# Where the products of the 64-key remainders with v stand in an attention and feed-forward kernel, and where their weights are kept

## The chip, the cores and the metric

The kernel runs on one core of a Trainium2 chip. A core has a matrix engine (PE, with weight loads PEld beside its matmuls), a vector engine (DVE), a scalar engine (ACT), a third elementwise engine (POOL) and queues that issue transfers (here SP's). Each engine works through a list of its own in order; engines wait for one another by semaphores. The metric is the device time of one execution, in microseconds (us).

## The reference

Eight batches of twelve heads, 448 tokens, head width 64. Attention uses a sigmoid in place of a softmax; the heads side by side are the 768 columns of x, which goes through two matrix products with g = h - tanh(h) between them.

```python
def _attn_ref(q, k, v):
    scale = 1.0 / np.sqrt(q.shape[-1])
    scores = scale * np.matmul(q, k.transpose(0, 1, 3, 2)) - np.log(S)
    attn = 1.0 / (1.0 + np.exp(-scores))
    return np.matmul(attn, v).astype(np.float32)

def _moe_ref(x, w_in, w_out):      # (3584, 768) x (768, 2048) x (2048, 768)
    h = x @ w_in
    g = h - np.tanh(h)
    return (g @ w_out).astype(np.float32)
```

A sigmoid needs no sum over the keys, so the products of weights and v can be added up in any order, key block by key block.

## The kernel before

**Numbers.** Most products are made of two f16 halves of each f32 operand: high by high, low by high, high by low, three matmuls for one. The halves of the attention weights ("ahl") are made by `split_a`: the high one on ACT (L411), the low one on DVE (L412). From batch 2 on (`AV32 = 2`) the attention runs this way; batches 0 and 1 take v and the weights in f32.

**Pairs and key blocks.** Heads are taken two by two: pair j (0 to 5) of a batch fills 128 of x's columns, one head in each half. The 448 keys are three blocks of 128 (c = 0, 1, 2) and a remainder of 64 (c = QT = 3). The remainders of an even pair g and the odd pair h = g + 1 are computed together, so that the array is used as four parts of 64x64: `scores` with two pairs and `av` with two accumulators. The other scores use two parts of 64 rows by 128 columns, the other products with v two parts of 128 rows by 64 columns, and the matmuls of the feed-forward part the whole array.

**The attention as a stream.** `stream` is a generator that lays out the attention of batches 1 to 7. One turn of its loop handles two pairs g and h, in four steps between which it yields:

- step 1: scores of (g, 0) and (g, 1) and their sigmoids on ACT (`units`, `weigh`, L405); then `do_av`, the products with v that are in the list `todo`: (h, 0..2) of the turn before, after which that h is closed; then `keep` splits the two new blocks of weights; loads and the squares of v (`norm_v`, L335)
- step 2: scores of (g, 2) and of the remainder (g, QT), sigmoids, norms of k and q, splits
- step 3, behind a short piece with the scales of the next two pairs (`pbn`, L344): scores of (h, 0), (h, 1); `do_av` for (g, 0..2) and the remainder, which opens h's accumulator; g is closed; the halves of the next v's and k's; splits
- step 4: scores of (h, 2), sigmoid, split

Closing a pair (`close_acc`, `evac_x`) copies its accumulator to x on ACT (L439) and takes squares (`add_squares`): for j = 0 and 5 on ACT (L454), for the others a product on POOL (L456), and for j = 1 to 4 the running sum on POOL too (L465), the last of which is `x2b`. There are two accumulators in PSUM, one under the tag "av" for even pairs, which also holds `pbn`, and one under "tr" for odd pairs.

**The order around it.** `second(b)` runs the second feed-forward product of batch b (`moe2`, L857) unit by unit: a unit is six matmuls, sixteen units make one tile of 128 tokens, and 48 units the batch's three tiles; the remainder of 64 tokens (`por`, L905, two parts of 128x64) follows. A tile has two accumulators `po`, for the two halves of the columns, and there are two such buffers in all, so that the next tile begins when ACT (L890) and DVE (L894) have copied the last one out; in batch 1's first tile ACT makes both copies (L890, L892). `BLOCKS` says behind which unit the next step of the stream is laid out:

```python
BLOCKS = (8, 11, 16, 20, 20, 20, 27, 32, 36, 36, 36, 43, 48, 52, 52)
```

These are step 4 (8), 1 (11), 2 (16), the scales, 3 and 4 (20, 20, 20), 1 (27), 2 (32), scales, 3 and 4 (36), 1 (43), 2 (48), scales and 3 (52). Steps 2 thus stand where a token tile ends. The step behind unit 43 is the first of the next batch's attention, and it closes the last pair of the present one; three units later the sums over x's squares (`token_norms`, `nm`, L690) are laid out, and then x's halves (L723, L724). Batch 1 has a list with three more steps (4, 7, 8, 11, 13, 16, ...), in which step 1 comes at unit 13. The first feed-forward product (`moe1`, L773) has no attention beside it. The engines' lists are in this order, which is written out by hand.

**Room.** The tile `wo` holds w_out's halves, 32 slots of 768 f16 columns, and three slots more, through which the f32 numbers were moved while they were split; `scratch` gives parts of it by offset. Splits of weights otherwise take buffers of the common pool "t" (eight).

Of the kernel before, what the change touches and what calls it, by code (L numbers as in the profile page):

```python
# [8 lines left out]
F16 = mybir.dt.float16  # L9
# [10 lines left out]
P = 128  # L20
D = 64
QT = 3
# [11 lines left out]
class Builder:  # L34
# [286 lines left out]
    def load_v(self, b, j, pool, tag, bufs):  # L321


        at = 0 if j % 2 == 0 else 2 * QT + 2
        n = 2 * QT + (0 if j % 2 else 2)
        t = pool.tile([P, n, D], F32, name="vn", tag=tag, bufs=bufs)
        self.nc.sync.dma_start(t, self.v[b, j // 2, :, at : at + n])
        return t
# [76 lines left out]
        self.nc.scalar.activation(a[:, 0], ps[:, :, : self.S], AF.Sigmoid, bias=self.nls, scale=scale)  # L405
        return a

    def split_a(self, a):
        nc = self.nc
        A = self.tp.tile([P, 2, 2, self.S], F16, name="ahl", tag="t")  # L410
        nc.scalar.activation(A[:, 0], a[:, 0], AF.Copy, scale=A_SCALE)  # L411
        nc.vector.scalar_tensor_tensor(A[:, 1], a[:, 0], A_SCALE, A[:, 0], op0=ALU.mult, op1=ALU.subtract)  # L412
        return A

    def av(self, acc, v, A, c, odd):


        half = c == QT
        m = P // len(acc)
        prods = ((0, 0), (1, 0), (0, 1)) if A.dtype == F16 else ((0, 0),)  # L420
        for n, (w, x) in enumerate(prods):
            for i in range(len(acc)):
                for h in range(2):
                    k = slice(i * m, (i + 1) * m)
                    self.nc.tensor.matmul(  # L425
                        acc[i][h * D : (h + 1) * D, : self.S],
                        v[k, w, 2 * QT + h if half else h * QT + c],
                        A[k, x, h],
                        start=(n == 0 and (i == 1 if half else c == 0 and not odd)),
                        stop=(n == len(prods) - 1 and (i == 0 if half else c == QT - 1 and bool(odd))),  # L430
                    )

    def evac_x(self, j, acc, iv):
# [34 lines left out]
    def stream(self):  # L468

        NP = self.NP
        G = (self.B - 1) * NP
        at = lambda g: (1 + g // NP, g % NP)
        splits = lambda g: at(g)[0] >= self.AV32
        qk, vn, sc, K, Q, vv, accs = {}, {}, {}, {}, {}, {}, {}

        def load(g):
            if g < G and g not in qk:  # L480
                qk[g] = self.load_qk(*at(g))

        def load_v(g):
            if g < G and splits(g):
                vn[g] = self.load_v(*at(g), self.nat, "vn", 2)

        def sums(g):
            ss = self.sums[g // 2 % 2]
            return ss if splits(g) else ss[:, :4]

        def norms(g):
            if g < G:
                for n, t in enumerate(qk[g]):
                    self.norm(t, sums(g)[:, 2 * n + g % 2 : 2 * n + g % 2 + 1])

        def norm_v(g):
            if g in vn:
                self.norm(vn[g], sums(g)[:, 4 + g % 2 : 5 + g % 2])

        def scales(g, where):  # L500
            if g < G:
                sc[g] = sc[g + 1] = self.scales(sums(g), where)

        def parts_k(g):
            if g < G:
                K[g] = self.parts(qk[g][0], sc[g][0][:, 0:1], "K", not splits(g) and g not in (2, 3))

        def parts_q(g):
            if g < G:
                Q[g] = self.parts(qk[g][1], sc[g][0][:, 1:2], "Q", True)  # L510
                qk.pop(g)

        def prep_v(g):
            if g >= G:
                return
            if splits(g):
                vv[g] = self.prep_v(vn.pop(g), sc[g][0])
            else:
                vv[g] = self.load_v(*at(g), self.att, "vhl", 3)[:, None]

        load(0)
        load(1)
        yield 0, False
        norms(0)
        norms(1)
        yield 0, False
        scales(0, "tr")
        yield 0, False
        parts_k(0)
        yield 450, False  # L530
        parts_q(0)
        load(2)
        yield 450, False
        parts_k(1)
        yield 450, False
        parts_q(1)
        load(3)
        yield 450, False
        norms(2)
        yield 0, False  # L540
        todo = []

        def open_acc(g):
            tag = "tr" if g % 2 else "av"
            accs[g] = self.ps.tile([P, 512], F32, name="acc", tag=tag, bufs=1)
            if g % NP == 0:
                self.xs = []

        def close_acc(g):
            iv = sc[g][1][:, 1:2] if splits(g) else None  # L550
            self.xs.append(self.evac_x(g % NP, accs.pop(g), iv))
            if g % 2:
                vv.pop(g - 1)
                vv.pop(g)
            for d in (sc, K, Q):
                d.pop(g)

        def do_av():
            for g, c, A in todo:
                odd = g % 2  # L560
                if c == QT:
                    open_acc(g + 1)
                    self.av([accs[g], accs[g + 1]], vv[g], A, c, odd)
                    close_acc(g)
                    continue
                if c == 0 and not odd:
                    open_acc(g)
                self.av([accs[g]], vv[g], A, c, odd)
                if c == QT - 1 and odd:
                    close_acc(g)  # L570
            todo.clear()

        def units(g, cs, between=lambda: None):

            pss = []
            for c in cs:
                n = 2 if c == QT else 1
                pss.append(self.scores([K[g + i] for i in range(n)], [Q[g + i] for i in range(n)], c))
            aa = [self.weigh(pss[0], sc[g][1][:, 0:1])]
            between()  # L580
            aa += [self.weigh(ps, sc[g][1][:, 0:1]) for ps in pss[1:]]
            return aa

        def keep(g, cs, aa):
            if splits(g):
                aa = [self.split_a(a) for a in aa]
            todo.extend((g, c, a) for c, a in zip(cs, aa))

        for g in range(0, G, 2):
            h = g + 1  # L590
            early = g == 0

            aa = units(g, (0, 1))
            do_av()
            if early:
                prep_v(0)
                prep_v(1)
            keep(g, (0, 1), aa)
            load(g + 3)
            norm_v(g + 2)  # L600
            norm_v(g + 3)
            yield 2750, True

            aa = units(g, (2, QT))
            if early:
                do_av()
            norms(g + 3)
            keep(g, (2, QT), aa)
            yield 2750, True

            if not early:
                scales(g + 2, "av")
                parts_k(g + 2)
                yield 0, False

            aa = units(h, (0, 1), (lambda: None) if early else lambda: parts_q(g + 2))
            do_av()
            if early:
                yield 2750, True
                scales(g + 2, "mm")  # L620
                parts_k(g + 2)
                parts_q(g + 2)
            prep_v(g + 2)
            keep(h, (0, 1), aa)
            prep_v(g + 3)
            load(g + 4)
            load_v(g + 4)
            load_v(g + 5)
            yield 2750, True

            aa = units(h, (2,), lambda: parts_k(g + 3))
            if early:
                do_av()
            keep(h, (2,), aa)
            parts_q(g + 3)
            norms(g + 4)
            yield 2750, True
        do_av()
        yield 1150, True

    def attention32(self):
# [497 lines left out]
```

## Time and profile before

| | us |
|---|---|
| median of the runs | 1165.48 |
| lowest run | 1165.2 |
| the profiled execution | 1166.29 |
| its span, from the first to the last instruction | 1164.5 |
| mean granted TensorE clock | 0.999 |
| one turn of the attention loop, from step 1 to step 1 (574.29 to 599.07) | 24.8 |

The time line of an engine merges neighbouring instructions of one line. Its columns are the start, how long the group took, the engine, the line of the kernel, the operation, the tile written and the tiles read, the shape (for matmuls first the part of the array: rows by columns), and their count; in brackets stands the idle time ahead of the group and what ended it. Matmuls overlap, so a group's length is a little more than the distance to the next group's start.

### The profile page before, as it was taken

Reading aid. Unit: us, or ns where it says so; the run is one execution under the profiler, and the core shown is the slowest. Engines: PE = TensorE matmul, PEld = TensorE weight load, DVE = VectorE, ACT = ScalarE, POOL = GpSimd, SP = SyncE. Lnnn points to the kernel's source line nnn. Section 1 sums busy time; section 2 is a strip of 40 time slices with the busy share of each in tenths; the row PEclk is TensorE's granted clock in tenths of the full one; section 3 lists DMA queues with packets and bytes.
Section 4 is the critical chain, followed back from the end, with each engine's and each line's share of the span. In section 5 each row is a group of like instructions: output and inputs, shape, how many; then the busy total and the mean of one; then the engine's idle time right before and its main releaser. Section 6 shows DMA issues by size and latency. Waiting matters only on the chain.

```text
span 1164.5 us, 18896 instructions
## 1 busy us (share of the span) xinstructions
PE 1153.1 (99%) x7563; PEld 597.4 (51%) x7564; DVE 907.7 (78%) x1308; ACT 865.5 (74%) x1195; POOL 79.1 (7%) x58
## 2 busy tenths in 40 slices
PE   9999999999999999999999999999999999999998
PEld 3345444555555555555555555555555555555565
DVE  6999999789777996679867897778976798646930
ACT  7988996588976888768887688867887688745820
POOL 0000000000120002200021000200022000300000
PEclk9999999999999999999999999999999999999999
DMA  9942171000222002210022101210012100000000
GB/s 358 357 163 64 42 224 53 29 7 1 80 75 64 7 1 78 62 53 1 17 76 62 40 1 31 82 58 24 1 55 84 53 1 9 23 28 7 1 14 35
DMA packets 34056, 70.43 MB, mean 60 GB/s; under 512 B 3888, under 2 KB 21040, under 8 KB 33968
## 3 DMA queue, kind: packets, MB, share of 16 engines
q1 hardware_dynamic: 33744, 68.89, 18.1%
q8 instruction: 59, 0.97, 0.4%
q10 hardware_dynamic: 224, 0.33, 0.1%
q14 instruction: 29, 0.24, 0.1%
HBM read 58.20 MB, written 11.01 MB: 59 GB/s over the span
## 4 chain that ended last, share of the span: by engine, by line
PE 73%; ACT 1%; issue 0%; DVE 0%; ACTq 0%
PE ph L773 28%; PE po L857 27%; PE sc L394 6%; PE acc L425 6%; PE por L905 5%; ACT a L405 0%; ACT ahl L411 0%; PE nm L690 0%; ACT sqn L335 0%; ACT x L439 0%; ACT Q L369 0%; DVE orem L914 0%; PE pbn L344 0%; ACT x L454 0%; ACT o L892 0%
## 5 line engine op out<-in xcount | busy, mean ns | idle before, releaser
L857 PE MATMUL po<-wo,g 128*128 128x384 f16 x2304 | 389.1, 326 | 3.1 <-DVE wo L240 1.6
L773 PE MATMUL ph<-xhl,wi 128*128 128x448 f16 x2016 | 382.6, 352 | 0.0
L857 PEld LDWEIGHTS <-g 128*128 128x128 f16 x2304 | 220.3, 98 | 170.1 <-issue 26.4
L773 PEld LDWEIGHTS <-wi 128*128 128x128 f16 x2016 | 196.7, 98 | 185.0 <-issue 2.1
L412 DVE SCALAR_TENSOR_TENSOR ahl<-a,ahl 128x896 f16<-128x896 f32 x126 | 162.7, 1326 | 125.6 <-ACT ahl L411 125.0
L405 ACT ACTIVATE a<-sc,nls,rn 128x896 f32<-128x896 f32 x147 | 155.8, 1090 | 37.4 <-PE sc L394 37.2
L811 ACT ACTIVATE u<-ph,ih 128x896 f32<-128x896 f32 x64 | 64.4, 1006 | 75.8 <-PE ph L773 74.0
L411 ACT ACTIVATE ahl<-a 128x896 f16<-128x896 f32 x126 | 113.2, 941 | 0.6
L394 PE MATMUL sc<-Q,K 64*128 64x448 f16 x1008 | 100.8, 353 | 0.9 <-DVE th L816 0.7
L815 DVE SCALAR_TENSOR_TENSOR m<-ph,ihk,u 128x896 f32<-128x896 f32 x64 | 73.5, 1149 | 25.6 <-ACT th L813 25.2
L766 ACT ACTIVATE g<-m,Sg 128x896 f16<-128x896 f32 x64 | 66.7, 1041 | 35.5 <-DVE m L829 28.5
L829 DVE COPY_PREDICATED m<-u,th 128x896 f32<-128x896 uint32 x64 | 77.2, 1206 | 6.8 <-ACT u L828 0.8
L425 PE MATMUL acc<-ahl,vhl 128*64 128x448 f16 (+1 forms) x864 | 80.6, 356 | 0.4 <-ACT tn L346 0.4
L456 POOL TENSOR_TENSOR x<-x 128x448 f32<-128x448 f32 x24 | 28.3, 1178 | 762.1 <-ACT x L439 762.1
L767 DVE SCALAR_TENSOR_TENSOR g<-m,Sg,g 128x896 f16<-128x896 f32 x64 | 73.4, 1147 | 6.8 <-ACT g L766 6.7
L826 DVE SCALAR_TENSOR_TENSOR m<-q,m 128x896 f32<-128x896 f32 x64 | 69.9, 1092 | 6.7 <-DVE m L822 0.5
L983 PE MATMUL ph<-x,wi 128*128 128x448 f32 x192 | 73.8, 540 | 0.0
L816 DVE SCALAR_TENSOR_TENSOR th<-ph,ih,th 128x896 f32<-128x896 f32 x64 | 73.3, 1145 | 0.0
L822 DVE SCALAR_TENSOR_TENSOR m<-q,m 128x896 f32<-128x896 f32 x64 | 69.6, 1087 | 0.0
L828 ACT ACTIVATE u<-u,b 128x896 f32<-128x896 f32 x64 | 66.7, 1042 | 1.9
L821 ACT ACTIVATE q<-u,b 128x896 f32<-128x896 f32 x64 | 65.8, 1028 | 0.0
L825 ACT ACTIVATE q<-u,b 128x896 f32<-128x896 f32 x64 | 65.8, 1028 | 0.0
(141 smaller groups left out, 1087.7 us busy)
## 6 DMA issues: line engine op xcount, KB each, us to landing
knn<-k SPq DMA_DIRECT2D x45, 224.0 KB, 2.6
qnn<-q SPq DMA_DIRECT2D x44, 224.0 KB, 2.6
rawo<-moe_w_out SPq DMA_DIRECT2D x22, 384.0 KB, 5.2
out<-o SPq DMA_DIRECT2D x21, 384.0 KB, 2.3
raw<-moe_w_in SPq DMA_DIRECT2D x13, 512.0 KB, 8.2
vn<-v SPq DMA_DIRECT2D x24, 256.0 KB, 2.8
wo<-moe_w_in SPq DMA_DIRECT2D x11, 512.0 KB, 8.3
vn<-v SPq DMA_DIRECT2D x24, 192.0 KB, 2.4
```

Of the source, the lines that this page charges most:

```text
L394: self.nc.tensor.matmul(ps[i * m : (i + 1) * m, h, : self.S], K[i][r, w, c * P : c * P + m], Q[i][r, x, :], start=(n == 0), stop=(n == len ...
L405: self.nc.scalar.activation(a[:, 0], ps[:, :, : self.S], AF.Sigmoid, bias=self.nls, scale=scale)
L411: nc.scalar.activation(A[:, 0], a[:, 0], AF.Copy, scale=A_SCALE)
L412: nc.vector.scalar_tensor_tensor(A[:, 1], a[:, 0], A_SCALE, A[:, 0], op0=ALU.mult, op1=ALU.subtract)
L425: self.nc.tensor.matmul(acc[i][h * D : (h + 1) * D, : self.S], v[k, w, 2 * QT + h if half else h * QT + c], A[k, x, h], start=(n == 0 and ...
L767: nc.vector.scalar_tensor_tensor(g[:, 1], m, Sg, g[:, 0], op0=ALU.mult, op1=ALU.subtract)
L773: self.nc.tensor.matmul(ph, self.wi[:, self.slot(c, k), part, e * P : (e + 1) * P], xhl[c][:, x, :], start=(i == 0), stop=(i == len(prods) ...
L815: V.scalar_tensor_tensor(m, ps, ihk, u, op0=ALU.mult, op1=ALU.mult)
L816: V.scalar_tensor_tensor(th, ps, ih, th, op0=ALU.mult, op1=ALU.subtract)
L829: V.copy_predicated(m, u.bitcast(U32), th)
L857: nc.tensor.matmul(po[i][:, :H], gs[f // 2][:, x, f % 2, tk * P : (tk + 1) * P], self.wo[:, i * self.NF + 2 * ks[f // 2] + f % 2, w], star ...
L983: nc.tensor.matmul(ph[:, e, :S], self.fp32(self.wi, self.slot(c, k))[:, 0, e * P : (e + 1) * P], xs[c], start=(c == 0), stop=(c == self.NC ...
```

## The change

From batch 2 on, the scores of the remainder (g, QT) move from step 2 to step 1, and the products of that remainder with v move from step 3 of the same turn to step 1 of the next turn, directly behind the remainder scores of the next two pairs, which use the array in the same four parts. Step 1 now has scores (g, 0); the products (h, 0..2) of the turn before; scores (g, QT); the remainder products of the turn before (`do_rest`), which close both of its pairs. Step 2 has scores (g, 1) and (g, 2). The weights of a remainder are used a turn after they are made; their halves lie in the three last slots of `wo`, in one place for all turns. The 64 remainder rows of v now lie with the odd pair's blocks (first six and then eight columns of 64, in place of eight and six), and the accumulation of a pair starts with block c = 0 and stops with the remainder.

```diff
     def load_v(self, b, j, pool, tag, bufs):
-        at = 0 if j % 2 == 0 else 2 * QT + 2
-        n = 2 * QT + (0 if j % 2 else 2)
+        first = 2 * QT + (2 if b < self.AV32 else 0)
+        at = j % 2 * first
+        n = 4 * QT + 2 - first if j % 2 else first
@@
-    def split_a(self, a):
-        nc = self.nc
-        A = self.tp.tile([P, 2, 2, self.S], F16, name="ahl", tag="t")
+    def split_a(self, a, kept):
+        nc = self.nc
+        if kept:
+            A = self.scratch((self.NF - self.SHIFT_O) * 2 * self.HALF, 4 * self.S).rearrange("p (x h n) -> p x h n", x=2, h=2)
+        else:
+            A = self.tp.tile([P, 2, 2, self.S], F16, name="ahl", tag="t")
@@
-    def av(self, acc, v, A, c, odd):
+    def av(self, acc, v, A, c, odd, late=False):
         half = c == QT
+        if late:
+            begin, end = (not half and c == 0,) * 2, (half,) * 2
+        else:
+            begin = (False, True) if half else (c == 0 and not odd,)
+            end = (True, False) if half else (c == QT - 1 and bool(odd),)
@@
-                        start=(n == 0 and (i == 1 if half else c == 0 and not odd)),
-                        stop=(n == len(prods) - 1 and (i == 0 if half else c == QT - 1 and bool(odd))),
+                        start=(n == 0 and begin[i]),
+                        stop=(n == len(prods) - 1 and end[i]),
@@
+        def do_rest():
+            while kept:
+                g, A = kept.pop()
+                self.av([accs[g], accs[g + 1]], vv[g + 1], A, QT, 0, True)
+                close_acc(g)
+                close_acc(g + 1)
+
         def do_av():
             for g, c, A in todo:
                 odd = g % 2
+                if splits(g):
+                    if c == 0:
+                        open_acc(g)
+                    self.av([accs[g]], vv[g], A, c, odd, True)
+                    continue
@@
         def keep(g, cs, aa):
             if splits(g):
-                aa = [self.split_a(a) for a in aa]
-            todo.extend((g, c, a) for c, a in zip(cs, aa))
+                aa = [self.split_a(a, c == QT) for c, a in zip(cs, aa)]
+            for c, a in zip(cs, aa):
+                if splits(g) and c == QT:
+                    kept.append((g, a))
+                else:
+                    todo.append((g, c, a))
@@
-            aa = units(g, (0, 1))
-            do_av()
+            first, second = ((0, QT), (1, 2)) if splits(g) else ((0, 1), (2, QT))
+            if splits(g):
+                aa = units(g, (0,))
+                do_av()
+                aa += units(g, (QT,))
+                do_rest()
+            else:
+                aa = units(g, first)
+                do_av()
@@
-            keep(g, (0, 1), aa)
+            keep(g, first, aa)
@@
-            aa = units(g, (2, QT))
+            aa = units(g, second)
@@
-            keep(g, (2, QT), aa)
+            keep(g, second, aa)
@@
         do_av()
+        do_rest()
```

Outside the chip the array v is laid out in the matching order before it is passed in.

More of the change, by code (lines that the diff above doesn't have):

```diff
@@ L540, in stream @@
         yield 0, False
-        todo = []
+        todo, kept = [], []
         def open_acc(g):
@@ L1122 @@
     rest = v[:, :, QT * P :].reshape(B, H // 4, 2, 2, D, D).transpose(0, 1, 2, 4, 3, 5).reshape(B, H // 4, P, 2, D)
+    n = Builder.AV32
+    v_first = np.concatenate([heads[:n, :, :, 0], rest[:n], heads[:n, :, :, 1]], axis=3)
+    v_later = np.concatenate([heads[n:, :, :, 0], heads[n:, :, :, 1], rest[n:]], axis=3)
     arrays = {
@@ L1125 @@
         "k": pairs(k),
-        "v": np.ascontiguousarray(np.concatenate([heads[:, :, :, 0], rest, heads[:, :, :, 1]], axis=3)),
+        "v": np.concatenate([v_first, v_later]),
         "moe_w_in": np.ascontiguousarray(moe_w_in).view(np.uint64),
```

## The prediction

> **What bounds the kernel now.** I read the page's busy times first, then the table of windows, then the waits, and last each engine's time line around one turn of the attention loop.
>
> ```profile
> PE 1153.1 (99%) x7563; PEld 597.4 (51%) x7564; DVE 907.7 (78%) x1308; ACT 865.5 (74%) x1195; POOL 79.1 (7%) x58
> 500.00:600.00 100.00, 100.00 (x660) 52.68 (x656) 85.71 (x114) 76.44 (x97) 6.12 (x4) 1.00 0.10 30
> ```
>
> In the window row the columns behind the length are PE, PEld, DVE, ACT, POOL, clock, DMA share and GB/s: PE is at work for all of these 100 us, at the full clock. So the change can act in two ways only: PE's own work gets shorter or longer, or PE is made to wait where it waits for nothing today. Moving work between the other engines costs nothing until one of them is late for PE.
>
> **The change part by part.** *The shapes on PE.* The number of matmuls stays. What changes is how often PE goes from one array shape to another: full (w_out's products), 64 rows (scores, "S"), 64 columns (products with v, "A"), 64x64 (both remainders, "R").
>
> ```profile
> 574.29 1.31 PE L394 MATMUL sc<-Q,K 64*128 64x448 f16 x12
> ...
> 582.33 1.43 PE L394 MATMUL sc<-Q,K 64*128 64x448 f16 x18
> ...
> 588.95 2.58 PE L425 MATMUL acc<-ahl,vhl 128*64 128x448 f16 x30
> 591.47 0.74 PE L394 MATMUL sc<-Q,K 64*128 64x448 f16 x6
> 592.14 7.00 PE L857 MATMUL po<-wo,g 128*128 128x384 f16 x42
> 599.07 1.31 PE L394 MATMUL sc<-Q,K 64*128 64x448 f16 x12
> 600.31 1.89 PE L425 MATMUL acc<-ahl,vhl 128*64 128x448 f16 x18
> 602.13 5.05 PE L857 MATMUL po<-wo,g 128*128 128x384 f16 x30
> 607.12 1.43 PE L394 MATMUL sc<-Q,K 64*128 64x448 f16 x18
> 608.48 4.08 PE L857 MATMUL po<-wo,g 128*128 128x384 f16 x24
> ```
>
> From start to start, 12 S take 1.24 us (599.07 to 600.31) and 6 S take 0.67 (591.47 to 592.14), so six more cost 0.57 and a stretch of its own 0.10. 18 A take 1.82, which is 3 x 0.57 + 0.11. The 30 of 588.95 are 18 A and 12 R, 2.52: the R cost 0.70, that is 0.57 + 0.13; the 18 of 607.12 are 6 S and 12 R, 1.36, and give 0.69. One change of shape costs 0.10 to 0.13; I take 0.12. The new order has one meeting without a row, A followed by S (steps 3 and 4); it is bounded by these ends.
>
> Changes of shape in a turn: before, step 1 has 3 (S A full), step 2 has 3 (S R full), steps 3 and 4 have 5 (S A R S full); after, 4 (S A R full), 2 and 4. One fewer. Where a batch's remainder tokens (L905, the shape of A) surround steps 2 and 3, which is so in the first turn of batches 3 to 7, it is two fewer. The last remainder of all needs one more. 18 turns: 12 x 1 + 1 (batch 2's first) + 5 x 2 - 1 = 22, times 0.12 = 2.6 us saved. Within a turn step 1 grows by 0.70 (12 R for 6 S, and 12 more R), step 2 shrinks by 0.13, steps 3 and 4 by 0.69.
>
> *What else moves to step 1.* Both pairs of the turn before are now closed there: two copies of x on ACT (L439) and up to four POOL instructions (L456, L465) come together, where before the even pair's stood in step 3. The second sigmoid now waits on ACT for R scores which stand behind A, and the copies and both splits (L411) are queued behind it. The split's other half on DVE (L412) collides with POOL, and behind it on DVE stands the copy of w_out's result (L894), for which PE's next token tile waits: `po` has two buffers, and both are in use. That is the chain to work out.
>
> ```profile
> 576.54 2.07 ACT L405 ACTIVATE a<-sc,nls,rn 128x896 f32<-128x896 f32 x2
> 578.50 0.62 ACT L439 ACTIVATE x<-acc,rn 128x448 f32<-128x448 f32 x1
> ...
> 599.85 2.09 ACT L405 ACTIVATE a<-sc,nls,rn 128x896 f32<-128x896 f32 x2 [2.32 <-PE sc L394]
> 602.24 0.64 ACT L439 ACTIVATE x<-acc,rn 128x448 f32<-128x448 f32 x1 [0.30 <-PE acc L425]
> 602.78 1.78 ACT L411 ACTIVATE ahl<-a 128x896 f16<-128x896 f32 x2
> ...
> 627.03 0.63 ACT L439 ACTIVATE x<-acc,rn 128x448 f32<-128x448 f32 x1 [0.30 <-PE acc L425]
> 627.75 0.58 ACT L454 ACTIVATE x<-x 128x448 bf16<-128x448 f32 x1
> ```
> ```profile
> 166.71 1.14 POOL L465 TENSOR_TENSOR x<-x,x 128x448 f32<-128x448 f32 x1 [9.15 <-ACT x L454]
> ...
> 579.27 0.94 POOL L456 TENSOR_TENSOR x<-x 128x448 f32<-128x448 f32 x1 [96.08 <-ACT x L439]
> 580.28 1.86 POOL L465 TENSOR_TENSOR x<-x,x 128x448 f32<-128x448 f32 x1
> ```
> ```profile
> 574.09 0.45 DVE L371 TENSOR_SCALAR K<-knn,sn 128x448 f16<-128x448 f32 x1
> ...
> 576.17 0.68 DVE L372 SCALAR_TENSOR_TENSOR Q<-qnn,sn,Q 128x448 f16<-128x448 f32 x1
> 580.00 3.09 DVE L412 SCALAR_TENSOR_TENSOR ahl<-a,ahl 128x896 f16<-128x896 f32 x2 [3.14 <-ACT ahl L411]
> 583.01 0.60 DVE L894 TENSOR_SCALAR o<-po,iK 128x384 f32<-128x384 f32 x1
> 587.19 2.09 DVE L412 SCALAR_TENSOR_TENSOR ahl<-a,ahl 128x896 f16<-128x896 f32 x2 [3.57 <-ACT ahl L411]
> ```
>
> Two splits on DVE take 2.09 us alone and 3.09 beside POOL, and POOL's sum takes 1.86 beside DVE and 1.14 where it went first: they take turns, and a split that waited ends 0.95 after POOL's instruction (580.28 + 1.86 = 582.14, and 580.00 + 3.09 = 583.09). ACT's next begins 1.0 after a sigmoid, 0.53 after an x, 0.85 after a split; POOL begins 0.14 after x ends.
>
> *Turn at 599.07 (step 1 behind unit 27).* A sigmoid starts 0.78 after its scores (599.85). R scores start at 599.07 + 0.67 + 1.82 = 601.56, their sigmoid at 602.37, the x copies at 603.37 and 603.90, the splits at 604.43 and 605.28, ending 605.38 and 606.23. POOL: product 604.14, sum 605.15 to 606.29. The first DVE split, ready at 605.4, ends at 607.2, POOL's next product at 608.0, the second split at 609.0, the copy L894 at 609.5. PE: step 2 starts at 607.12 + 0.70 = 607.82, the next tile at 609.06, its second product at 609.22. A wait of 0.3 us; six times, 1.9.
>
> *Turn at 574.29 (behind unit 11).* ACT is later from the start (576.54). R sigmoid 577.58, first x 578.58, its square on ACT (j = 0; 0.09 behind x, 0.58), second x 579.8 to 580.4, splits to 581.25 and 582.1. POOL's product runs 580.54 to 581.48, the split ends 582.4, POOL's sum 583.4, the second split 584.4, L894 584.9; PE wants it at 582.33 + 0.70 + 1.24 + 0.16 = 584.43. A wait of 0.5; five times, 2.5. Q's low half for the R scores (L372, to 576.85) is just in time for their second product (574.29 + 2.49 + 0.21 = 576.99): nothing, at most 0.1 a turn if late.
>
> ```profile
> 623.85 1.31 PE L394 MATMUL sc<-Q,K 64*128 64x448 f16 x12
> ...
> 629.85 0.35 PE L690 MATMUL nm<-x2b,onesb 128*128 128x448 bf16 x1
> ```
>
> *Turn at 623.85 (behind unit 43).* The sums nm of line 690 need POOL's last sum, which today follows step 3 and is long done. After: R sigmoid 623.85 + 2.49 + 0.81 = 627.15, x 628.15 to 628.78, product 628.92, sum 629.94 to 631.08 (DVE has nothing ready to collide). PE is there at 629.85 + 0.70 = 630.55: a wait of 0.6, five times, 3.0; the last batch has no sigmoid in front, 0.15.
>
> ```profile
> 301.07 1.31 PE L394 MATMUL sc<-Q,K 64*128 64x448 f16 x12
> ```
> ```profile
> 302.79 2.07 ACT L405 ACTIVATE a<-sc,nls,rn 128x896 f32<-128x896 f32 x2
> ...
> 308.07 0.57 ACT L890 ACTIVATE o<-po,iK 128x384 f32<-128x384 f32 x1
> 308.54 0.58 ACT L892 ACTIVATE o<-po,iK 128x384 f32<-128x384 f32 x1
> ```
>
> *Batch 1's first tile.* Step 1 comes at unit 13, three units before the tile ends, and both copies of the result are on ACT. The R sigmoid starts at about 301.07 + 2.49 + 0.81 = 304.4 at the earliest, where today's second starts at 303.8, and an x and a square (0.53 + 0.6) come in between: 1.7 us later, while PE is 0.6 later. Net 1.1 to 1.7 with late Q halves; I take 1.5.
>
> *At no cost:* the loads of v (same bytes, swapped between the pairs, a turn ahead); the kept halves in w_out's room, written in step 1 and read by PE a turn (24.8 us) later, their reader of the turn before being through before the R sigmoid ends; one buffer of the common pool fewer in use.
>
> *Sum:* -2.6 + 1.9 + 2.5 + 3.15 + 1.5 = +6.5 us. The profiled execution took 1166.29 (span 1164.5), which becomes 1172.8; on the median 1165.48, 0.8 below it, 1172.0. The waits have ends: 0.2 to 0.8 behind unit 11, 0 to 0.6 behind 27, 0.4 to 0.8 at nm, 0.6 to 2 in batch 1, so 3.7 to 13.6 together, and +1 to +11 net.
>
> *A rule weighed.* L894 reads PSUM and never lies beside POOL here. Its 0.60 for 384 elements is slower than L371's 0.45 for 448 from SBUF, which speaks for another way of reading; behind unit 27 POOL's last sum is waiting just then, and if L894 had to take its turn it would end 0.95 later. I take none of it. The Trainium skill, SBUF — State Buffer, section "Who interferes with whom", says that a DVE instruction with at most one SBUF input outside the two-port modes does not contend with GpSimd; by it the sum is my +6.5, without it +12.2; no run here shows it yet.
>
> **The rivals.** (1) *The waits don't arise, only the saved changes count:* 1165.5 - 2.6 = 1162.9. For it: the waits are 0.3 to 0.6, small beside the 3 to 5 us chains they are worked out from. Against it: at nm PE needs a chain of sigmoid, x and two POOL instructions that ends 0.6 late without any collision. (2) *L894 takes turns with POOL:* six times 0.95 more, 1177.7. (3) *PE waits for the kept halves although it doesn't read them*, because they are written into the tile wo which every product of w_out reads: then the first product behind step 1 waits for the second split, 609.0 - 602.83 = 6.2 us in the turn at 599.07, 18 times, less 2.6: 1274, slower. It decides from 1.4 us a turn (2% is 23.3). Against it stand products that ran unbroken while DVE wrote other parts of wo:
>
> ```profile
> 191.64 5.50 PE L857 MATMUL po<-wo,g 128*128 128x384 f16 x31
> ```
> ```profile
> 191.82 0.62 DVE L239 TENSOR_SCALAR wo<-wo,swo_s 128x768 f16<-128x768 f32 x1
> ...
> 194.18 1.77 DVE L240 SCALAR_TENSOR_TENSOR wo<-wo,swo_s 128x768 f16<-128x768 f32 x1
> ```
>
> **How the numbers follow.** Forecast 0.60, rival 1 0.20, rival 2 0.13, rival 3 0.05, and 0.02 for what I don't see, half to each side. A measurement of this kernel tells about 2% from no change. Forecast and rivals 1 and 2 lie within it: 0.93; slower 0.06, faster 0.01, since nothing on PE but 2.6 us can go away. The forecast's own range is 1166 to 1177; with rivals 1 and 2 it is 1162.5 to 1179.
>
> **What would show it.** Right: in a turn's time line step 1 as 6 S, 18 A, 24 R with a distance of 3.76 us, steps 3 and 4 as S A S; in the waits, PE `po` behind DVE `o` L894 of 0.3 to 0.5 us at the tile ends, and PE `nm` behind POOL L465 of about 0.6. Wrong: PE unbroken at these places (rival 1); waits over 1.2 us behind unit 27 (rival 2); PE idle for microseconds behind every step 1 (rival 3); or a meeting of A and S that costs far more than 0.13.

## The result, and the profile after

| | before | changed |
|---|---|---|
| median of the runs, us | 1165.61 | 1178.6 |
| lowest run, us | 1165.2 | 1177.78 |
| span of the profiled execution, us | 1164.5 | 1176.8 |
| ratio to before, 95% interval | | 1.0113 (1.0102 to 1.0124) |

The change made the kernel 1.1% slower, 12.3 us by the spans, where 6.5 us were forecast. The time 1178.6 lies outside the forecast's own range (1166 to 1177) and inside only the one that was widened for rivals 1 and 2 (to 1179); the loss is almost twice the forecast, so one or more terms were wrong or missing. With further runs of the kernel before, its median is 1165.61 here, where it was 1165.48 above. (The line numbers of the changed kernel are a few to some thirty higher: L394 is L395 there, L405 L406, L412 L416, L425 L433, L454 L462, L465 L473, L690 L722, L692 L724, L857 L889, L894 L926.)

The page's first row of the changed kernel, and from its waits the rows of PE that the kernel before doesn't have (total us, times, longest):

```profile
PE 1155.4 (98%) x7563; PEld 599.8 (51%) x7564; DVE 890.2 (76%) x1308; ACT 866.5 (74%) x1195; POOL 69.1 (6%) x58
```
```profile
PE po L889 <- DVE o L926: 2.9, 11, 0.6
PE sc L395 <- DVE m L724: 2.6, 5, 0.5
PE nm L722 <- POOL x2b L473: 2.1, 5, 0.4
...
PE nm L722 <- ACT x L462: 1.6, 6, 0.3
PE po L889 <- ACT o L922: 1.3, 1, 1.3
```

PE does the same 7563 matmuls. It now waits in five kinds of places. Two were not forecast at all: PE's scores behind DVE's reduction of nm (L724), and nm behind a square on ACT (L462). These idle times are smaller than the losses, since a matmul is drawn over the start of the next; a loss is read from the distance of two starts, against the same distance where nothing waits. The time line of PE in the changed kernel, the turn behind unit 11 and its tile end:

```profile
581.01 0.76 PE L395 MATMUL sc<-Q,K 64*64 64x448 f16 x12
581.61 0.74 PE L433 MATMUL acc<-wo,vhl 64*64 64x448 f16 x12
582.27 5.05 PE L889 MATMUL po<-wo,g 128*128 128x384 f16 x30
587.26 1.31 PE L395 MATMUL sc<-Q,K 64*128 64x448 f16 x12
588.50 0.34 PE L889 MATMUL po<-wo,g 128*128 128x384 f16 x1
589.13 3.90 PE L889 MATMUL po<-wo,g 128*128 128x384 f16 x23 [0.29 <-DVE o L926]
```

The two kinds of remainder stand behind each other and PE goes straight on to w_out's products (582.27). At the tile end the second product starts 0.63 behind the first, where 0.16 is the distance without a wait: 0.47 lost, forecast 0.5. Now the turn behind unit 43:

```profile
632.38 3.10 PE L889 MATMUL po<-wo,g 128*128 128x384 f16 x18
635.89 0.35 PE L722 MATMUL nm<-x2b,onesb 128*128 128x448 bf16 x1 [0.41 <-POOL x2b L473]
636.50 0.35 PE L722 MATMUL nm<-x,onesb 128*128 128x448 bf16 x1 [0.26 <-ACT x L462]
636.69 2.11 PE L889 MATMUL po<-wo,g 128*128 128x384 f16 x12
638.73 0.74 PE L395 MATMUL sc<-Q,K 64*128 64x448 f16 x6
640.00 0.74 PE L395 MATMUL sc<-Q,K 64*128 64x448 f16 x6 [0.53 <-DVE m L724]
```

From 632.38 to nm it is 3.51, against 2.93 before (626.92 to 629.85): 0.58 for POOL's sum, forecast 0.6. Then the second nm is 0.61 behind the first (0.19 without a wait), 0.42 lost, and the second score block is 1.27 behind the first (0.57), 0.70 lost. These 1.1 us a batch are what the forecast lacks. The time lines of ACT, POOL and DVE at that place, changed kernel:

```profile
632.94 1.15 ACT L447 ACTIVATE x<-acc,rn 128x448 f32<-128x448 f32 x2
635.87 0.58 ACT L462 ACTIVATE x<-x 128x448 bf16<-128x448 f32 x1 [1.79 <-POOL x2b L473]
636.35 0.93 ACT L415 ACTIVATE ahl<-a 128x896 f16<-128x896 f32 x1
```
```profile
633.70 0.93 POOL L464 TENSOR_TENSOR x<-x 128x448 f32<-128x448 f32 x1 [19.17 <-ACT x L447]
634.71 1.13 POOL L473 TENSOR_TENSOR x2b<-x,x 128x448 bf16<-128x448 f32 x1
```
```profile
637.32 1.09 DVE L416 SCALAR_TENSOR_TENSOR ahl<-a,ahl 128x896 f16<-128x896 f32 x1 [8.60 <-ACT ahl L415]
638.33 1.09 DVE L416 SCALAR_TENSOR_TENSOR wo<-a,wo 128x896 f16<-128x896 f32 x1
639.33 0.62 DVE L724 TENSOR_REDUCE m<-nm 128x1 f32<-128x448 f32 x1
```

Both x were copied by 634.09, but ACT's square of pair 5 starts at 635.87, just behind POOL's sum (634.71 + 1.13 = 635.84), although it does not read that sum. In the code the squares x2 have two buffers. One is the running sum, the other holds pair 4's product; the square of pair 5 can have one only when POOL's last sum has read both. ACT stands still for 1.79 us with both splits behind the square; DVE's splits are as late, the reduction of nm behind them ends at 639.95, and PE's second score block, which takes the buffer of "sc" that nm used, starts at 640.00. Before, POOL's sum was long done (618.67 + 1.86 = 620.53) when the square came (627.75, a row of the prediction), and DVE's reduction started 1.4 us behind the first nm (629.85), where it is now 3.4 us (635.89 to 639.33):

```profile
618.67 1.86 POOL L465 TENSOR_TENSOR x2b<-x,x 128x448 bf16<-128x448 f32 x1
```
```profile
629.20 2.09 DVE L412 SCALAR_TENSOR_TENSOR ahl<-a,ahl 128x896 f16<-128x896 f32 x2 [4.06 <-ACT ahl L411]
631.21 0.62 DVE L692 TENSOR_REDUCE m<-nm 128x1 f32<-128x448 f32 x1
```

Theory: the loss is a sum of separate waits, each for work of step 1 that is late by less than 1.5 us, and the two that were missed hang on the two buffers of x2. The rivals to it stand with the experiments.

### The profile page after: what moved, and what is told of

It reads as the page before. It is cut to its first block, busy times and chain, and to the rows that moved or that the text cites. A ratio compares the mean times of both kernels' runs of the same rounds, so it can differ in the third digit from the quotient of the medians.

```text
span 1176.8 us, 18881 instructions
## 1 busy us (share of the span) xinstructions
PE 1155.4 (98%) x7563; PEld 599.8 (51%) x7564; DVE 890.2 (76%) x1308; ACT 866.5 (74%) x1195; POOL 69.1 (6%) x58
## 4 chain that ended last, share of the span: by engine, by line
PE 63%; ACT 4%; DVE 3%; issue 3%; POOL 1%; DMA 0%; POOLq 0%; DVEq 0%; ACTq 0%
PE ph L805 28%; PE po L889 20%; PE acc L433 5%; PE sc L395 5%; PE por L937 5%; DVE wo L416 2%; ACT a L406 1%; ACT x L447 1%; ACT ahl L415 1%; DVE o L926 1%; POOL x2b L473 0%; POOL x L464 0%; ACT x L462 0%; DMA qnn<-q 0%; DVE m L724 0%
## 5 line engine op out<-in xcount | busy, mean ns | idle before, releaser
L889 PE MATMUL po<-wo,g 128*128 128x384 f16 x2304 | 390.7, 326 | 6.7 <-DVE o L926 2.9
L889 PEld LDWEIGHTS <-g 128*128 128x128 f16 x2304 | 220.2, 98 | 177.9 <-issue 35.4
L416 DVE SCALAR_TENSOR_TENSOR ahl<-a,ahl 128x896 f16<-128x896 f32 x108 | 119.6, 1135 | 154.0 <-ACT ahl L415 154.0
L406 ACT ACTIVATE a<-sc,nls,rn 128x896 f32<-128x896 f32 x147 | 158.2, 1091 | 55.8 <-PE sc L395 54.9
L395 PE MATMUL sc<-Q,K 64*128 64x448 f16 (+1 forms) x1008 | 103.0, 353 | 3.6 <-DVE m L724 2.6
L415 ACT ACTIVATE ahl<-a 128x896 f16<-128x896 f32 x108 | 98.1, 941 | 0.6
L433 PE MATMUL acc<-ahl,vhl 128*64 128x448 f16 x648 | 68.3, 355 | 0.5 <-ACT tn L347 0.4
L857 ACT ACTIVATE q<-u,b 128x896 f32<-128x896 f32 x64 | 65.8, 1028 | 0.0
```

The lines of the kernel that those rows point to most:

```text
L395: self.nc.tensor.matmul(ps[i * m : (i + 1) * m, h, : self.S], K[i][r, w, c * P : c * P + m], Q[i][r, x, :], start=(n == 0), stop=(n == len ...
L433: self.nc.tensor.matmul(acc[i][h * D : (h + 1) * D, : self.S], v[k, w, 2 * QT + h if half else h * QT + c], A[k, x, h], start=(n == 0 and ...
L889: nc.tensor.matmul(po[i][:, :H], gs[f // 2][:, x, f % 2, tk * P : (tk + 1) * P], self.wo[:, i * self.NF + 2 * ks[f // 2] + f % 2, w], star ...
```

## The experiments

Six kernels were run. Each ratio is to runs of the kernel before that were made beside it (median 1166.19 for the first four, 1165.82 for the last two). Spans are those of the profiled executions; the runs of one kernel differ by up to 3 us, so a loss is read place by place in the time line, and a few tenths of a span say little. Line numbers are those of the changed kernel or up to five more.

### Three buffers for the squares

A tile in another part of the program shares these buffers and gets the same count.

```diff
-                pool, tag, bufs = (self.xp, "x2", 2) if p["k"] % 3 == 1 else (self.nat, "vn", 2)
+                pool, tag, bufs = (self.xp, "x2", 3) if p["k"] % 3 == 1 else (self.nat, "vn", 2)
@@
-        x2 = self.xp.tile([P, self.S], BF16 if last else F32, name="x2", tag="x2", bufs=2)
+        x2 = self.xp.tile([P, self.S], BF16 if last else F32, name="x2", tag="x2", bufs=3)
```

> The changed kernel with three buffers in place of two for the squares x2. Theory (ACT's square of the last pair waits for a buffer that POOL's last sum still reads, and both splits, the copies and DVE's reduction of nm stand behind it): the wait of nm's second matmul (0.42 us, six times) and that of the second score of step 2 behind unit 48 (0.69 us, five times) go, 6.0 us, span 1176.8 to 1170.8; nm's first wait (0.57) and those at the tile ends (0.47 and 0.35) stay. Rival (these splits are late because the second sigmoid waits for the remainder scores, and the reduction stands behind them whatever the square does): the 0.69 stays and only 0.42 x 6 = 2.5 us go, 1174.3. Rival (the square waits for POOL's data, not for room): nothing changes, 1176.8.

Measured: 1171.84 us, 1.0050 of before (1.0036 to 1.0064), span 1169.9. ACT and PE of this kernel at the same place:

```profile
630.13 1.15 ACT L447 ACTIVATE x<-acc,rn 128x448 f32<-128x448 f32 x2
631.37 0.58 ACT L462 ACTIVATE x<-x 128x448 bf16<-128x448 f32 x1
```
```profile
633.02 0.35 PE L722 MATMUL nm<-x2b,onesb 128*128 128x448 bf16 x1 [0.35 <-POOL x2b L473]
633.21 0.35 PE L722 MATMUL nm<-x,onesb 128*128 128x448 bf16 x1
...
635.44 1.31 PE L395 MATMUL sc<-Q,K 64*128 64x448 f16 x12
```

The square follows its x at once, the second nm its first by 0.19, and the twelve scores run unbroken. Both missed waits are gone in every batch, 6.0 us by the distances of starts, as expected: they come from the room for x2. The span is 6.9 us shorter; of the other 0.9, about 0.4 lies ahead of batch 2's attention and 0.4 at the first nm, where the waits are 0.51 and 0.07 in place of 0.57 and 0.13. Both rivals are refuted; in particular the late remainder scores alone don't delay the reduction enough.

### Without POOL's squares

```diff
         last = j == self.NP - 1
+        if pool and not last:
+            if j == 0:
+                self.x2 = self.xp.tile([P, self.S], BF16, name="x2b", tag="x2b", bufs=1)
+                nc.scalar.activation(self.x2, x, AF.Square, scale=3.0)
+            return
```

> The changed kernel without the squares of pairs 1 to 4 in the batches that split their weights: POOL's products and sums there are left out, and the squares of pair 0, times nine, and of pair 5 stand for all. Theory (DVE's splits take turns with POOL, and nm and the last square wait for POOL): the waits at the tile ends (0.47 behind unit 11's step and 0.35 behind unit 27's) go as well as those at nm and behind unit 48, 13.4 us in all, span about 1163.4; two splits on DVE take 2.1 us everywhere. Rival (ACT's later start of the splits alone makes DVE's copy late): the tile ends keep 0.3 to 0.5 us each, 4.4 us, span about 1168.

Measured: 1164.56 us, 0.9988 of before (0.9978 to 0.9997), span 1162.8. DVE behind unit 27, first of the changed kernel with its POOL, then of this one:

```profile
609.96 1.84 DVE L416 SCALAR_TENSOR_TENSOR ahl<-a,ahl 128x896 f16<-128x896 f32 x1 [6.35 <-ACT ahl L415]
611.73 1.81 DVE L416 SCALAR_TENSOR_TENSOR wo<-a,wo 128x896 f16<-128x896 f32 x1
613.47 0.60 DVE L926 TENSOR_SCALAR o<-po,iK 128x384 f32<-128x384 f32 x1
```
```profile
610.93 1.66 POOL L464 TENSOR_TENSOR x<-x 128x448 f32<-128x448 f32 x1
612.68 1.86 POOL L473 TENSOR_TENSOR x<-x,x 128x448 f32<-128x448 f32 x1
```
```profile
604.66 1.09 DVE L416 SCALAR_TENSOR_TENSOR ahl<-a,ahl 128x896 f16<-128x896 f32 x1 [5.89 <-ACT ahl L415]
605.67 1.08 DVE L416 SCALAR_TENSOR_TENSOR wo<-a,wo 128x896 f16<-128x896 f32 x1
607.17 0.62 DVE L931 TENSOR_SCALAR o<-po,iK 128x384 f32<-128x384 f32 x1 [0.42 <-PE po L894]
```

With POOL each split takes 1.8, without it 1.09, and DVE's copy then waits for PE instead of PE for it. In batches 2 to 7 none of the five waits is left. So the tile ends are lost to the turns that DVE and POOL take, not to ACT's later start alone. This kernel also shows what the new order brings when nothing is late in these batches: 1.7 us below the span of before, with batch 1's 1.45 still in it.

### Steps laid out earlier, in both kernels

The last four lines keep the sums nm, and the scales and halves of x behind them, behind the units where they were.

```diff
-    BLOCKS = (8, 11, 16, 20, 20, 20, 27, 32, 36, 36, 36, 43, 48, 52, 52)
+    BLOCKS = (7, 10, 16, 20, 20, 20, 25, 32, 36, 36, 36, 41, 48, 52, 52)
-    BLOCKS1 = (4, 7, 8, 11, 13, 16, 20, 20, 20, 27, 32, 36, 36, 36, 43, 48, 52, 52)
+    BLOCKS1 = (4, 7, 8, 10, 12, 16, 20, 20, 20, 25, 32, 36, 36, 36, 41, 48, 52, 52)
@@
-            events.append((end + 3, norms))
-            events += [(p, lambda: next(scales[0], None)) for p in (end + 5, end + 7)]
+            events.append((end + 5, norms))
+            events += [(p, lambda: next(scales[0], None)) for p in (end + 7, end + 9)]
```

> The changed kernel with step 1 laid out behind units 10, 25 and 41 in place of 11, 27 and 43 (step 4 behind 7 in place of 8, batch 1's steps 4 and 1 behind 10 and 12 in place of 11 and 13), the sums nm and x's halves behind the same units as now. Theory (every loss is a wait for work of step 1 that comes 0.3 to 1.3 us late, the shapes themselves save about 3 us): the waits of 13.4 us in batches 2 to 7 go and part of batch 1's 1.9; span 1162 to 1163.5, below the 1164.5 of the kernel before. Rival (the new order of step 1 costs PE itself): the waits go but the span stays above 1166. Rival (the wait only moves: step 1's products and remainder scores are now early for the splits and for Q's halves of step 4): new waits at acc or sc, span 1165 to 1172.

> The kernel before with the same earlier places of steps 4 and 1 as the other run of this kind. Theory (the kernel before has no waits that these places could take away, 1.9 us in all): 1164 to 1165 span, no change, so that what the other run gains is the change's. Rival (the earlier places are a gain of their own): 1 to 3 us below.

Measured: the changed kernel 1168.73 us, 1.0023 (1.0013 to 1.0033), span 1167.3; the kernel before 1167.17, 1.0012 (1.0003 to 1.0021), span 1165.9. For the changed kernel the theory missed (1162 to 1163.5 expected) and the second rival came true; the kernel before is 0.9 us above its expected 1164 to 1165. PE and ACT of the changed kernel with the earlier steps:

```profile
574.90 1.71 PE L433 MATMUL acc<-ahl,vhl 128*64 128x448 f16 x16
577.07 0.38 PE L433 MATMUL acc<-ahl,vhl 128*64 128x448 f16 x2 [0.46 <-DVE ahl L416]
```
```profile
572.70 1.04 ACT L798 ACTIVATE g<-m,Sg 128x896 f16<-128x896 f32 x1 [2.96 <-DVE m L861]
573.65 1.08 ACT L406 ACTIVATE a<-sc,nls,rn 128x896 f32<-128x896 f32 x1
```

The waits at nm, behind unit 48 and at the tile ends behind units 16 and 32 are gone, but the products (h, 2) of step 1 now wait 0.6 us for step 4's split, in each of batches 2 to 6. That split did not come earlier with its step: its sigmoid stands on ACT behind the last g of the first product, which waits for DVE. In batch 1 the same wait is 1.25 us. Moving the steps alone makes the kernel before 0.1% slower (its products with v lose 1.2 us more, 0.73 of it in one wait of batch 1), so what the changed kernel gains by it is no gain of the places as such. DVE and PE of the kernel before with the earlier steps:

```profile
576.12 1.08 DVE L412 SCALAR_TENSOR_TENSOR ahl<-a,ahl 128x896 f16<-128x896 f32 x1
```
```profile
575.64 2.00 PE L425 MATMUL acc<-ahl,vhl 128*64 128x448 f16 x18
```

The split ends at 577.20 here, hardly later than in the changed kernel, where PE goes on at 577.07. But the products stand behind twelve scores here and begin at 575.64, where in the changed kernel they stand behind six and begin at 574.90; here they lose about 0.1 us. So the new order itself asks for this split earlier, by the 0.57 us of six scores at least, and leaves less room on both sides of step 1: laid out late, its work is late for the tile ends and nm, and laid out early, it waits for step 4.

### Three buffers and two places; then copies before squares

From the kernel with three buffers: step 1 behind units 25 and 41, but behind 11 as it was, and the offsets of the sums as in the section above.

```diff
-    BLOCKS = (8, 11, 16, 20, 20, 20, 27, 32, 36, 36, 36, 43, 48, 52, 52)
+    BLOCKS = (8, 11, 16, 20, 20, 20, 25, 32, 36, 36, 36, 41, 48, 52, 52)
-    BLOCKS1 = (4, 7, 8, 11, 13, 16, 20, 20, 20, 27, 32, 36, 36, 36, 43, 48, 52, 52)
+    BLOCKS1 = (4, 7, 8, 11, 13, 16, 20, 20, 20, 25, 32, 36, 36, 36, 41, 48, 52, 52)
```

> Three buffers for the squares, and step 1 behind units 25 and 41 in place of 27 and 43 (sums nm and halves of x behind the same units as in the changed kernel); the step behind unit 11 stays, since there the run with earlier places found a wait of 0.6 us for the split of step 4. Theory (each wait has its own place and cause): of the waits of the run with three buffers, 0.28 to 0.29 us at the tile end behind unit 32 (six) and 0.51 at nm (five) go, 4.3 us; the one at the tile end behind unit 16 (0.53, five) stays: span 1169.9 to 1165.6. Rival (the waits hang together, and those taken away come back at the next place): 1168 or more.

Measured: 1168.01 us, 1.0020 (1.0011 to 1.0029), span 1165.8, 1165.6 expected (the profiled execution is one of the shorter of its eleven). The waits at nm and behind unit 32 are gone, the 0.53 behind unit 16 stays, and none comes back elsewhere. Then also, with a second argument to `close_acc` that leaves the squares out of the copy:

```diff
-                close_acc(g)
-                close_acc(g + 1)
+                close_acc(g, True)
+                close_acc(g + 1, True)
+                for i in range(2):
+                    self.add_squares((g + i) % NP, self.xs[(g + i) % NP], True)
```

> The same, and in the remainder step both accumulators are copied before the squares are taken, so that pair 0's square (ACT, 0.6 us) no longer stands between the two copies. Theory: POOL's product begins 0.6 us earlier, the collision with the first split is over earlier, DVE's copy is 0.4 us earlier and the wait behind unit 16 falls from 0.53 to 0.1: span 1163.5, below the kernel before (1164.5). Rival (the splits' start on ACT decides, not POOL): the wait stays at 0.5 and the span at 1165.6.

Measured: 1165.71 us, 1.0000 of before (0.9991 to 1.0008), span 1164.1. ACT and PE of this kernel:

```profile
578.81 1.15 ACT L447 ACTIVATE x<-acc,rn 128x448 f32<-128x448 f32 x2
579.84 0.58 ACT L463 ACTIVATE x<-x 128x448 f32<-128x448 f32 x1
```
```profile
584.48 4.20 PE L892 MATMUL po<-wo,g 128*128 128x384 f16 x24
...
588.62 1.31 PE L395 MATMUL sc<-Q,K 64*128 64x448 f16 x12
```

The copies stand together. The 24 products behind unit 16 with `pbn` take 4.14 from start to start, those behind unit 32, which wait for nothing, 4.01 (609.26 to 613.27): some 0.13 is left of the 0.53, as expected. Every loss in batches 2 to 7 but this is taken back, and the kernel is level with the one before, not below it as was expected. Of what the shapes save, 1.3 us go at batch 1's first tile and 0.7 at the tile ends behind unit 16; what should be left is too small for these runs to show.

## Why the prediction was wrong

The direction was right and so were the chains that the prediction worked out, but one chain was followed too short, and half of the loss was missing. Term by term, with what the changed kernel's time line shows:

| term | forecast, us | measured, us |
|---|---|---|
| changes of shape on PE | -2.6 | -2.9 (what is left of the sum; 0.3 of it lies ahead of the first step that moved, which begins at 204.17, before at 204.47) |
| tile end behind unit 16 | +2.5 | 4 waits of 0.47 and one of 0.82: +2.7 |
| tile end behind unit 32 | +1.9 | 6 of 0.35: +2.1 |
| first nm, for POOL's sum | +3.15 | 5 of 0.57 and 0.13: +3.0 |
| batch 1's first tile | +1.5 | 1.17 more at the tile end, 0.28 at products with v: +1.45 |
| second nm, for ACT's square | 0 | 6 of 0.42: +2.5 |
| second score block behind unit 48, for DVE's reduction | 0 | 5 of 0.69: +3.45 |
| sum | +6.5 | +12.3 |

*The step that failed* is "Turn at 623.85 (behind unit 43)". It followed POOL's chain to nm and stopped there ("The sums nm of line 690 need POOL's last sum"). It did not carry the square of pair 5 on ACT, though its own row at 627.75 shows it there just behind the copy of x, nor the reduction of nm on DVE, and the paragraph "At no cost" looked only at the common pool and the kept halves, not at the two buffers of x2. Before, step 3 closed pair 4 and step 1 pair 5, some 11 us apart, and two buffers were enough; closing both at once made the second square wait for the first pair's sum. ACT's list carried that 1.8 us on to the splits, DVE's list to the reduction, and the scores' buffer to PE: 5.95 us that the sum lacked. Three buffers took both waits away (6.0 of the 6.9 us by which the span fell), which shows the cause.

*What held.* The saving by shapes can be read from whole batches. The starts of the first feed-forward product in batches 2 and 4, before and after (the counts of the last two rows are those of the stretch that was asked for):

```profile
370.84 54.65 PE L773 MATMUL ph<-xhl,wi 128*128 128x448 f16 x288
...
645.55 54.65 PE L773 MATMUL ph<-xhl,wi 128*128 128x448 f16 x288
```
```profile
373.08 2.25 PE L805 MATMUL ph<-xhl,wi 128*128 128x448 f16 x11
```
```profile
651.78 3.39 PE L805 MATMUL ph<-xhl,wi 128*128 128x448 f16 x17
```

Two batches took 274.71 and take 278.70: 137.36 and 139.35 each. The five waits of a batch are 0.47 + 0.35 + 0.57 + 0.42 + 0.69 = 2.50, so PE's own work is 0.51 shorter; forecast were four changes of shape, 0.48. Three of the four chains, through two to four engines each, met their waits within 0.1 us, but for the one of 0.82, and within 0.2 us in their totals. This was not luck of the sum: DVE's copy behind unit 27 was forecast to end at 609.5, counted from a step 1 at 599.07; in the changed kernel that step begins 4.56 us later (603.63) and the copy ends at 614.07, which is 609.51 counted the same way. Batch 1's total came out by luck in part: 0.28 of its 1.45 lie at products with v, where no wait was forecast, and the tile end loses less than the 1.5. Why one wait behind unit 16 is 0.82 stays open. Rival 1 (no waits) is refuted by the waits, rival 3 (PE waits for the kept halves) by the products that begin at 582.27 without idle time. Rival 2 (L894 takes turns with POOL) is refuted by DVE's copy at 613.47, which takes its usual 0.60 inside POOL's sum of 612.68 to 614.54. Its price, 1177.7 us or +12.2, lies close to what was measured by coincidence.

## What to carry to other kernels

When two pieces of work that stood apart are laid out together, list every buffer that each piece takes, not only the data it reads: a pool that was large enough for them one after the other becomes a wait, and an engine's list hands that wait on to all that is queued behind it. Follow each engine's list past the first consumer, down to the next buffer that the busiest engine needs. Where an engine is at work 99% of the time, a saving in its own work, here 0.5 us a batch, is lost as soon as one neighbour is that late; here five were.

## What the runs showed of the hardware

The time line of PE in the changed kernel, with two meetings of shapes that had no row before:

```profile
594.20 1.89 PE L433 MATMUL acc<-ahl,vhl 128*64 128x448 f16 x18
596.03 0.74 PE L395 MATMUL sc<-Q,K 64*128 64x448 f16 x6
...
646.05 1.89 PE L433 MATMUL acc<-ahl,vhl 128*64 128x448 f16 x18
647.78 4.07 PE L937 MATMUL por<-wo,g 128*64 128x384 f16 x48
```

18 products followed by scores take 1.83 from start to start, as before any other shape; followed by matmuls of the same array shape they take 1.73, so there the 0.10 is not paid, although the line, the operands and the PSUM tile change. The Trainium skill, TensorEngine Tiling (Array Packing), section "Key Properties", says that a change of the tiling mode, and not just of the tile, drains the engine. These rows agree so far as the 0.10 is paid only where the array's parts change; that it is a drain they don't show.

The Trainium skill, SBUF — State Buffer, section "Who interferes with whom", says that a DVE instruction with at most one SBUF input, outside the two-port modes, does not contend with GpSimd (POOL), and that one with two SBUF inputs contends with a GpSimd instruction that reads SBUF. The trace agrees: DVE's copy out of PSUM took its usual 0.60 us beside POOL's sum (613.47), while the splits, which read two tiles in SBUF, took 1.8 in place of 1.09.
